# Four one-sign units become two two-sign units in a fused Fourier mixing and SoLU kernel on one core

## The chip, the cores and the metric

The kernel runs on one core of a Trainium2 chip. The metric is the time of one execution in device microseconds; shown is the median of several runs. The profile is of one execution, and its times are counted from the first instruction.

The engines are named as in the profile: PE is TensorE, DVE is VectorE, ACT is ScalarE, POOL is GpSimd, SP is SyncE, which here only issues DMAs. Each of them carries out its instructions in the order in which the program hands them over.

## The reference

```python
def _attn_ref(x):                      # x: 8 x 3136 x 256
    X = np.fft.fft(x, axis=1)
    X = np.fft.fft(X, axis=2)
    return X.real.astype(np.float32)

def _moe_ref(x, w_in, w_out, g_ln):    # x: 25088 x 256, d_ff 1024
    h = x @ w_in
    h_max = np.max(h, axis=-1, keepdims=True)
    e = np.exp(h - h_max)
    sm = e / (np.sum(e, axis=-1, keepdims=True) + 1e-09)
    solu = h * sm
    mu = np.mean(solu, axis=-1, keepdims=True)
    var = np.mean((solu - mu) ** 2, axis=-1, keepdims=True)
    ln = (solu - mu) / np.sqrt(var + 1e-06) * g_ln
    return (ln @ w_out).astype(np.float32)
```

The real part of a two-dimensional Fourier transform of each of 8 batches is taken as 25088 rows of 256, and each row goes through an up projection to 1024, a softmax times its own argument, a normalisation and a down projection to 256. All in float32.

## The kernel before

The sequence length is 3136 = 49 x 64. A frequency is k1 + 49 k2, with k1 from 0 to 48 and k2 from 0 to 63. The transform over 49 (`transform1`) and the transform over 64 with twiddle factors (`transform2`) run on PE. The batches are taken in four pairs.

**Units.** A unit is one pair of batches and one k1: 2 x 64 = 128 rows, one per partition. Since the input is real, the row of frequency -k follows from that of k: both have the same part even in the feature index and opposite odd parts. So k1 runs only from 0 to 24 (`NK` = 25), and a unit with k1 above 0 handles its rows with both signs of the odd part: 256 output rows. For k1 = 0 the mirrored rows lie in the same unit, so that unit has one sign: 128 output rows. There are 100 units, 96 with two signs and 4 with one (0, 25, 50 and 75).

**What a unit does.** PE multiplies its transform `q` by the folded input weights into two PSUM tiles `h0` and `h1` (`up`, L289). DVE adds the middle column to the first (`even`, L302, the column `r` having been spread over the partitions by a small DMA, L264) and makes the sums and differences with the second (`join`, L310, one per sign). ACT takes the exponential (`expo`, L318), DVE the product (`product`, L325), ACT the sum of squares (`square`, L332). Both signs lie in one tile `both`. DVE transposes it in blocks of 32 (`turn_both`, L396) into `v`, and sixteen DMAs per two units, issued by SP, place the blocks in `uT` (`move_blocks`, L432). POOL forms sums of quarters of `uT` (`sums`, L465), and PE multiplies by the output weights in seven products of quarters (`Down`, L472). ACT and DVE scale the results out of PSUM, and DMAs of SP (first sign, L567 and L569) and POOL (second sign, L559) store them. ACT copies one intermediate result inside PSUM as a start value ahead of the sixth of the seven products (`seed`, L498). A one-sign unit multiplies in the plain way (`down`, L542), without POOL's sums.

**Two units are a batch** (class `Batch`; not a batch of the input). A batch that is `shared` keeps the two units' blocks side by side so that the output leaves in larger DMAs. The first two batches, the last one, and every one with a one-sign unit are not shared.

**The order** is written out by hand, as one loop. In step i the engines work on the up projection of unit i, the second transform of unit i + 2 and the down projection of unit i - 5. In every even step the blocks of the two units before are moved. The first five steps (0 to 4) have an order of their own, in which PE transposes the units (`turn_whole`) instead of DVE and the DMAs; unit 0's down projection is in step 5. While one pair's units run, the first transform of the next pair runs in half pieces, at steps that the table `SUMS` names; the loads, folds and the four-part turn of its result (`turn`, POOL's DMAs into `g`) stand at steps counted from `NK`. The kernel ends with a last batch that is moved in smaller pieces.

The lines that set this rhythm:

```python
units = [Unit(p, k1) for p in range(NP) for k1 in range(NK)]
SUMS = [None] + [[f + 2 * c for c in range(NC)] for f in (3, 27, 53)]
# in step i, after the sums of POOL:
if i % 2 == 0 and whole < i - 1 < len(units) - 2:
    batches[i//2 - 1].place()
    move_blocks(batches[i//2 - 1], slice(0, 2))
```

Of the kernel before, what the change touches and what calls it, by code (L numbers as in the profile page):

```python
# [21 lines left out]
NK = N1 // 2 + 1  # L22
NH = N2 // 2
# [12 lines left out]
MIDDLE = (5,)  # L36
BY_PE = (0, 2)


def shared(b, n):  # L40

    return WHOLE // 2 <= b < n - 1 and all(u % NK for u in (2 * b, 2 * b + 1))


@with_exitstack
def kernel(
# [29 lines left out]
    out_k = out.rearrange("(p k2 k1) d -> p k1 k2 d", p=NP, k1=N1)  # L76

# [18 lines left out]
    ones = const.tile([P, P], FP32, name="ones")  # L96
    ident = const.tile([P, P], FP32, name="ident")
    neg_half = const.tile([P, 2], FP32, name="neg_half")
    idx = const.tile([P, NP * (NC + NK)], I32, name="idx")
    w_mid = const.tile([P, FF], FP32, name="w_mid")  # L100
    g_ln = const.tile([P, KF], FP32, name="g_ln")
    wbar = const.tile([P, D], FP32, name="wbar")
    top_bit = const.tile([P, 1], I32, name="top_bit")
# [139 lines left out]
    def transform2(pr, k1, bank=0):  # L243
# [3 lines left out]
        i, k = divmod(k1, KG)  # L247
        g = pr.g[i]
        table = T[0][:, :, k, :] if i == 0 else T[1][:, :, k1 - KG, :]
# [18 lines left out]
    class Unit:  # L268


        def __init__(self, p, k1):
            self.p, self.k1 = p, k1
            self.signs = (0, 1) if k1 else (0,)
            self.h, self.u, self.ot = [None] * 2, [None] * 2, [None] * 2
# [8 lines left out]
    def up(t, c):  # L283

        ps = ps_h.tile([P, FF], FP32, tag=f"h{c}", name=f"ps_h{c}")
        whole_even = c == 0 and t.p == 0 and t.k1 in MIDDLE
# [9 lines left out]
    def even(t, ps):  # L296

        t.ev = fpool.tile([P, FF], FP32, tag="ev", name="ev", bufs=1)
        if t.p == 0 and t.k1 in MIDDLE:
            nc.scalar.copy(t.ev, ps)  # L300
            return
# [19 lines left out]
    def product(t, s):  # L321

        if s == 0:
# [36 lines left out]
    class Batch:  # L360


        def __init__(self, b):
            self.first, self.shared = 2 * b, shared(b, NP * NK // 2)
# [38 lines left out]
    def turn_whole(t, late=False):  # L403
# [4 lines left out]
        for s in t.signs:  # L408
            for half in range(2):
                ps = result(2 * s + half + 1).rearrange("p (c k) -> p c k", c=n)  # L410
# [4 lines left out]
                if s or late:  # L415
# [138 lines left out]
    def store(t, s):  # L554

        dmas = []
        if s:
            i = NP * NC + t.p * NK + t.k1
# [4 lines left out]
        elif t.batch.shared:  # L563
            for j in range(4 if t.w else 0):
                a, w = divmod(j, 2)
                rows = out_k[t.p, t.k1 - 1 + w, 64 * a : 64 * a + 64].rearrange("(h n) d -> n h d", h=2)
                dmas.append(nc.sync.dma_start(out=rows, in_=t.batch.out[32 * j : 32 * j + 32]))  # L567
        else:
            dmas.append(nc.sync.dma_start(out=out_k[t.p, t.k1], in_=t.ot[s]))  # L569
# [197 lines left out]
    SUMS = [None] + [[f + 2 * c for c in range(NC)] for f in (3, 27, 53)]  # L767

    def ahead(pr, i, work, after=None):

        for c in range(NC):
            a = i - SUMS[pr.p][c]
            if work == "load" and (i == (pr.p - 1) * NK and c < 2 and (c or pr.p == 1) or a == 2 and c + 2 < NC):
                load(pr, c if a != 2 else c + 2)
# [11 lines left out]
    def ahead_pe(pr, i):  # L786

        for c in range(NC):
            half = i - SUMS[pr.p][c] - 2
            if c == 0 and pr.p == 2:  # L790
                halves = {1: (0, 1)}.get(half, ())
            else:
                halves = (half,) if half in (0, 1) else ()
# [388 lines left out]
```

## Time and profile before

| what | value |
|---|---|
| median of 3 runs | 1116.52 us (1116.32 to 1117.78) |
| profiled execution: span from first to last instruction | 1115.0 us (the profile gives no other time of it) |
| PE busy | 1098.1 us, 98% of the span |
| DVE, ACT, POOL busy | 976.0, 798.3, 808.6 us |
| first up projection starts | 48.26 us |
| step 5 starts | 78.23 us |
| up projection of the last unit starts | 1068.68 us |
| mean granted PE clock | 0.998 |

The 40 slices of the page show PE at 9 tenths or more from the third slice to the last but one. Where PE never waits, a step is as long as its instructions on PE; where it waits, the profile names what ended the wait. A table of windows gives for each stretch its length, then the busy time and number of instructions of PE, PEld, DVE, ACT and POOL, then the granted PE clock, the DMA engines' share and GB/s.

### The profile page before, as it was taken

To read this page: it belongs to the slowest core of one execution; us is meant where nothing else is said; L and a number is where in the kernel's file an instruction comes from. 1 tells how busy PE (TensorE), PEld (TensorE's weight loads), DVE (VectorE), ACT (ScalarE), POOL (GpSimd) and SP (SyncE) were. 2 spreads that over 40 slices of the span, in tenths; PEclk is the share of its full clock that TensorE was granted. 3 is DMA by queue.
4 is the path that set the end of the run, shared out by engine and by line. 5 is a ranking of instruction groups with operands and counts; after the bars stand their busy time and mean duration, and the time that the engine had idled before them with its cause. 6 is when DMAs were issued, how large, how long until landed. Compare 5 with 4: busy or idle time off the path is not lost. (4 is left out here: it accounts for less than half of the span.)

```text
span 1115.0 us, 22065 instructions
## 1 busy us (share of the span) xinstructions
PE 1098.1 (98%) x7063; PEld 877.4 (79%) x7063; DVE 976.0 (88%) x1432; ACT 798.3 (72%) x1947; POOL 808.6 (73%) x709
## 2 busy tenths in 40 slices
PE   8899999999999999999999999999999999999998
PEld 5558787888887878788788778787887788778888
DVE  7998889898888988989889989898898898998884
ACT  5598777777767777777767777777776777777772
POOL 4168888867876979766878878885775676766665
PEclk9999999999999999999999999999999999999999
DMA  9655987757968979765898888776696785865665
GB/s 338 216 175 135 185 206 176 175 135 152 193 155 180 200 181 198 177 151 130 157 176 176 194 185 197 183 174 150 139 163 141 142 169 113 163 141 114 141 132 129
DMA packets 457930, 187.76 MB, mean 168 GB/s; under 512 B 424646, under 2 KB 439254, under 8 KB 457816
## 3 DMA queue, kind: packets, MB, share of 16 engines
q1 hardware_dynamic: 443800, 146.94, 62.1%
q0 software_dynamic: 14016, 39.40, 12.9%
q8 instruction: 58, 0.95, 0.4%
q14 instruction: 56, 0.46, 0.1%
HBM read 46.75 MB, written 38.80 MB: 77 GB/s over the span
## 5 line engine op out<-in xcount | busy, mean ns | idle before, releaser
L289 PE MATMUL ps_h<-Wi,q 128*128 128x512 f32 x800 | 361.6, 593 | 0.4 <-DVE nmax L310 0.2
L465 POOL TENSOR_TENSOR S<-uT 128x512 f32<-128x512 f32 x186 | 237.3, 1276 | 110.9 <-DVE u L325 35.9
L472 PE MATMUL ps_m<-Ws,S 128*128 128x128 f32 x2304 | 296.0, 275 | 0.0
L472 PEld LDWEIGHTS ps_m<-Ws,S 128*128 128x128 f32 x2304 | 279.5, 192 | 3.2 <-issue 0.2
L332 ACT ACTIVATE h<-u,usum 128x1024 f32<-128x1024 f32 x196 | 225.0, 1148 | 73.5 <-DVE u L325 67.3
L289 PEld LDWEIGHTS ps_h<-Wi,q 128*128 128x128 f32 x800 | 144.2, 190 | 144.9 <-issue 141.9
L325 DVE SCALAR_TENSOR_TENSOR u<-h,u 128x1024 f32<-128x1024 f32 x196 | 234.9, 1234 | 10.9 <-ACT u L318 10.8
L318 ACT ACTIVATE u<-h,nmax 128x1024 f32<-128x1024 f32 x196 | 223.3, 1141 | 2.4 <-DVE nmax L310 1.1
L396 DVE STREAM_TRANSPOSE v<-u 128x2048 f32<-128x2048 f32 x88 | 203.4, 2311 | 3.1
L472 PE MATMUL ps_m<-Wo,uT 128*128 128x128 f32 x1536 | 203.7, 276 | 0.0
L472 PEld LDWEIGHTS ps_m<-Wo,uT 128*128 128x128 f32 x1536 | 187.9, 192 | 1.0 <-issue 1.0
L310 DVE CUSTOM_DVE_ANT_0 h<-ev,ps_h 128x1024 f32<-128x1024 f32 x100 | 122.1, 1221 | 17.0 <-DVE ev L302 9.1
L310 DVE CUSTOM_DVE_ANT_0 h<-h,ps_h 128x1024 f32<-128x1024 f32 x96 | 117.2, 1221 | 14.2 <-ACT ot L516 0.5
L559 POOL DMA_INDIRECT out_dram<-ot,idx x96 | 109.0, 1135 | 27.0 <-issue 11.9
L465 POOL TENSOR_TENSOR S<-uT,S 128x512 f32<-128x512 f32 x93 | 118.8, 1277 | 7.2
L465 POOL TENSOR_TENSOR S<-S,uT 128x512 f32<-128x512 f32 x93 | 118.6, 1276 | 7.3
L302 DVE SCALAR_TENSOR_TENSOR ev<-w_mid,r,ps_h 128x1024 f32<-128x1024 f32 x99 | 122.8, 1241 | 0.3
L472 PE MATMUL ps_m<-Ws,uT 128*128 128x128 f32 x768 | 101.8, 276 | 0.0
L472 PE MATMUL ps_m<-Wo,S 128*128 128x128 f32 x768 | 101.4, 275 | 0.0
L253 PEld LDWEIGHTS ps_m<-T,g 128*128 128x128 f32 x400 | 60.0, 191 | 48.1 <-issue 45.9
L507 ACT ACTIVATE ot<-ps_m,rs 128x256 f32<-128x256 f32 x96 | 45.4, 473 | 71.0 <-PE ps_m L472 50.7
L472 PEld LDWEIGHTS ps_m<-Ws,uT 128*128 128x128 f32 x768 | 93.8, 192 | 0.0
(122 smaller groups left out, 1218.1 us busy)
## 6 DMA issues: line engine op xcount, KB each, us to landing
uT<-v SPq DMA_DIRECT2D x752, 128.0 KB
g<-zd POOLq DMA_DIRECT2D x72, 160.0 KB, 4.5
out_dram<-ot SPq DMA_DIRECT2D x176, 64.0 KB
zd<-z SPq DMA_DIRECT2D x24, 400.0 KB
xa<-in_x_dram SPq DMA_DIRECT2D x24, 392.0 KB
raw_in<-in_moe_w_in_dram SPq DMA_DIRECT2D x4, 512.0 KB
xa<-in_x_dram SPq DMA_DIRECT2D x4, 512.0 KB
room<-in_x_dram SPq DMA_DIRECT2D x4, 512.0 KB
```

The lines of the kernel that those rows point to most:

```text
L253: nc.tensor.matmul(o, g[:, k, h * P : (h + 1) * P], table, start=(h == 0), stop=True, skip_group_check=True)
L289: nc.tensor.matmul(ps[:, fs], t.q[:, c * P : (c + 1) * P], Wi[:, c, fs], start=True, stop=not whole_even)
L302: nc.vector.scalar_tensor_tensor(out=t.ev, in0=w_mid, scalar=t.r, in1=ps, op0=ALU.mult, op1=ALU.add)
L310: nc.vector.tensor_tensor_reduce(out=t.h[s], in0=t.h[0] if s else t.ev, in1=t.odd, scale=1.0 if s else -0.5, scalar=3.0e38, op0=ALU.add, o ...
L318: nc.scalar.activation(out=t.u[s], in_=t.h[s], func=ACT.Exp, bias=t.nmax[:, s : s + 1], scale=-1.0, accum_out=t.esum[:, s : s + 1])
L325: t.last = nc.vector.scalar_tensor_tensor(out=t.u[s], in0=t.h[s], scalar=-1.0, in1=t.u[s], op0=ALU.mult, op1=ALU.mult, accum_out=t.usum[:, ...
L332: nc.scalar.activation(out=t.h[s], in_=t.u[s], func=ACT.Square, bias=t.usum[:, s : s + 1], scale=-float(FF), accum_out=t.ssq[:, s : s + 1])
L396: nc.vector.transpose(out=t.batch.v[:, :, t.w], in_=t.both.rearrange("p s (g n) -> p (s g) n", n=32))
L465: i = engine.tensor_tensor(out=S[j], in0=a, in1=b, op=op)
L472: nc.tensor.matmul(o, a[:, c], b[:, c], start=start and c == 0, stop=c == n - 1, skip_group_check=True)
L507: nc.scalar.mul(out=self.t.ot[1], in_=self.PP, mul=self.rs[1])
L559: dma = nc.gpsimd.indirect_dma_start(out=out, out_offset=bass.IndirectOffsetOnAxis(ap=idx[:, i : i + 1], axis=0), in_=t.ot[s], in_offset=None)
```

## The change

The four units with k1 = 0 go. Their rows are gathered into two units with two signs. In the pair tables k1 = 0 is moved to the end (index 24, `NU`); each pair has 24 ordinary units. At steps 24, 46, 70 and 86 (`SELF_STEPS`) an extra second transform yields the k1 = 0 rows of one pair; ACT copies k2 = 0 to 31 of both its batches into one half of a tile kept for them (`q_self`, in the place of `wbar` and of `ones` and `ident`, whose readers have finished), and k2 = 32, frequency 1568, which is its own mirror, into `q_half`. Two units, each with four batches by 32 frequencies, stand at places 90 and 91 (`SELF_AT`). Frequency 0 is its own mirror too; so in the second sign the rows of partitions 0, 32, 64 and 96 are free, and the eight rows of frequency 1568 go there. These eight rows run alone on 8 partitions in steps 87 to 89 (class `Half`), and DMAs of SP copy four of them into the tile `both` of each of the two units, between its product of the second sign, which now comes first, and its transpose. Their statistic is copied in the same way.

There are 98 units, all with two signs. All batches but the first two and the last are shared. Unit 0 has two signs in the steps of the start; its down projection stays plain, once for each sign.

The diff, cut to this (the tables of factors and of row numbers follow the new order and are left out):

```diff
+NU = NK - 1
+SELF_AT = 90
+SELF_STEPS = (24, 46, 70, 86)
 def shared(b, n):
-    return WHOLE // 2 <= b < n - 1 and all(u % NK for u in (2 * b, 2 * b + 1))
+    return WHOLE // 2 <= b < n - 1
+def order_of(NP):
+    units = [(p, k, None) for p in range(NP) for k in range(NU)]
+    units[SELF_AT:SELF_AT] = [(NP - 1, NU, m) for m in range(NP // 2)]
+    return units
...
-            self.signs = (0, 1) if k1 else (0,)
+            self.signs, self.usum = (0, 1), None
...
     def turn_whole(t, late=False):
-                ps = result(2 * s + half + 1).rearrange("p (c k) -> p c k", c=n)
+                bank = (1, 2, 0, 1)[2 * s + half] if late else 2 * s + half + 1
+                ps = result(bank).rearrange("p (c k) -> p c k", c=n)
...
-                if s or late:
+                if s or late and half:
                     t.wait.append((uT[:, half * n : (half + 1) * n, :, s], ps))
...
-    SUMS = [None] + [[f + 2 * c for c in range(NC)] for f in (3, 27, 53)]
+    SUMS = [None] + [[f + 2 * c for c in range(NC)] for f in (3, 26, 50)]
...
+    def gather_self(p):
+        ps = transform2(pairs[p], NU).rearrange("p (h b k) -> p h b k", h=KD, b=2)
+        of, b = q_self[p // 2].rearrange("p (h b k) -> p h b k", h=KD, b=4), p % 2 * 2
+        nc.scalar.copy(of[:, :, b : b + 2], ps[..., 0:NH])
+        nc.scalar.copy(q_half[:, :, 2 * p : 2 * p + 2], ps[..., NH])
+    class Half:
+        def spread(self):
+            nc.sync.dma_start(out=self.row[:, 0:1], in_=q_half[0:1, 1])
+        def up(self):
+            self.ps = ps_h.tile([P, FF], FP32, tag="h0", name="ps_h0")[0:B]
+            # two matmuls of q_half[:, 0] with Wi[:, 0]
+        def even(self): ...      # DVE, 8 x 1024, into a tile of xpool
+        def join(self): ...      # DVE
+        def expo(self): ...      # ACT
+        def product(self): ...   # DVE
+        def square(self): ...    # ACT
+        def stats(self): ...     # ACT, two small ones
+        def give(self, t, to, of):
+            nc.sync.dma_start(out=to, in_=of[4 * t.m : 4 * t.m + 4])
+        def give_u(self, t):
+            self.give(t, t.both[0 : P : NH, 1], self.u)
+        def give_v(self, t):
+            self.give(t, t.v[0 : P : NH, 1:2], self.row[:, 5:6])
...
         def by_seven(i):
-            return 0 <= i < len(units) and len(units[i].signs) == 2
+            return 1 <= i < len(units)
...
+            if i == NU - 3:
+                turn_parts(pairs[1], -3)
...
                 stats(prv)
+                if prv.m is not None:
+                    half.give_v(prv)
...
                 other_pairs(i, ahead_pe)
+                if i in SELF_STEPS:
+                    gather_self(SELF_STEPS.index(i))
+                if i == SELF_STEPS[-1]:
+                    half = Half()
+                    half.spread()
+                if i == SELF_STEPS[-1] + 1:
+                    half.up()
...
+            if i == SELF_STEPS[-1] + 1:
+                half.even()
+                half.join()
...
-                for s in cur.signs:
+                if i == SELF_STEPS[-1] + 2:
+                    half.expo()
+                for s in cur.signs if cur.m is None else (1, 0):
                     product(cur, s)
+                    if cur.m is not None and s:
+                        half.give_u(cur)
+                if i == SELF_STEPS[-1] + 2:
+                    half.product()
+                if i == SELF_STEPS[-1] + 3:
+                    half.square()
+                    half.stats()
```

Lines of the kernel after are 14 or more higher: L302 is L316, L310 is L324, L325 is L339, L332 is L346, L396 is L410, L432 is L447, L472 is L487.

Where the change puts its instructions is seen in the order of the built programs. First DVE at the start. Before, from unit 0's even part to unit 1's products (`ISA` is the join and the reading of its minimum):

```order
L302 SCALAR_TENSOR_TENSOR ev<-w_mid,r,ps_h_432 128x1024
L310 ISA h,nmax<-ev,ps_h_437 128x1024
L310 ISA nmax 128x1
L644 SCALAR_TENSOR_TENSOR Wo<-raw_out,g_ln,S_105 128x256 x2
L302 SCALAR_TENSOR_TENSOR ev<-w_mid,r,ps_h_453 128x1024
L325 SCALAR_TENSOR_TENSOR u,usum<-h,u 128x1024
L310 ISA h,nmax<-ev,ps_h_458 128x1024
```

And the same place now:

```order
L316 SCALAR_TENSOR_TENSOR ev<-w_mid,r,ps_h_432 128x1024
L324 ISA h,nmax<-ev,ps_h_437 128x1024
L324 ISA nmax 128x1
L324 ISA h,nmax<-h,ps_h_437 128x1024
L324 ISA nmax 128x1
L662 SCALAR_TENSOR_TENSOR Wo<-raw_out,g_ln,S_105 128x256 x2
L316 SCALAR_TENSOR_TENSOR ev<-w_mid,r,ps_h_456 128x1024
L339 SCALAR_TENSOR_TENSOR u,usum<-h,u 128x1024 x2
L324 ISA h,nmax<-ev,ps_h_461 128x1024
```

One more join stands ahead of unit 1's even part, and one more product ahead of its joins.

Second, DVE in step 87, from the even part of unit 87 to its transpose. Before:

```order
L302 SCALAR_TENSOR_TENSOR ev<-w_mid,r,ps_h_8484 128x1024
L310 ISA h,nmax<-ev,ps_h_8489 128x1024
L310 ISA nmax 128x1
L310 ISA h,nmax<-h,ps_h_8489 128x1024
L310 ISA nmax 128x1
L530 SCALAR_TENSOR_TENSOR ot_8421<-ps_m_102,rs_8209,ot_8421 128x128
L533 SCALAR_TENSOR_TENSOR ot_8498<-ps_m_104,rs_8209,ot_8498 128x256
L325 SCALAR_TENSOR_TENSOR u,usum<-h,u 128x1024 x2
L396 STREAM_TRANSPOSE v_8483<-u 128x64x32
```

Now (8x1024 are the eight rows; `ps_h_8795` lies in the same PSUM tile `h0` as the unit's own):

```order
L316 SCALAR_TENSOR_TENSOR ev<-w_mid,r,ps_h_8760 128x1024
L324 ISA h,nmax<-ev,ps_h_8765 128x1024
L324 ISA nmax 128x1
L324 ISA h,nmax<-h,ps_h_8765 128x1024
L324 ISA nmax 128x1
L545 SCALAR_TENSOR_TENSOR ot_8774<-ps_m_102,rs_8556,ot_8774 128x128
L548 SCALAR_TENSOR_TENSOR ot_8775<-ps_m_104,rs_8556,ot_8775 128x256
L844 SCALAR_TENSOR_TENSOR half<-w_mid,half,ps_h_8795 8x1024
L849 ISA half<-half 8x1024
L849 ISA half 8x1
L339 SCALAR_TENSOR_TENSOR u,usum<-h,u 128x1024 x2
L410 STREAM_TRANSPOSE v_8650<-u 128x64x32
```

The even part and the join of the eight rows stand behind the two rows that take the last products of the step out of PSUM, and ahead of the unit's own products.

Third, SP from step 88 to step 92. `uT<-v` x16 are the block moves of an even step, `out_dram<-ot` the stores of a batch, `r<-` the spread of a middle column. Before:

```order
L432 DMA uT<-v_8483 32x16x64 x16
L567 DMA out_dram<-ot_8606 32x2x256 x4
L264 DMA r<-q 128x1x1 x2
L432 DMA uT<-v_8668 32x16x64 x16
L567 DMA out_dram<-ot_8786 32x2x256 x4
L264 DMA r<-q 128x1x1 x2
L432 DMA uT<-v_8848 32x16x64 x16
```

Now (the moves of step 90 are those of `v_8843`):

```order
L585 DMA out_dram<-ot_8774 32x2x256 x4
L278 DMA r<-ones_ident 128x1x1
L278 DMA r<-q 128x1x1
L447 DMA uT<-v_8843 32x16x64 x16
L872 DMA u<-half 4x1024
L585 DMA out_dram<-ot_8956 32x2x256 x4
L278 DMA r<-q 128x1x1
L872 DMA own<-half 4x1
L872 DMA u<-half 4x1024
L278 DMA r<-q 128x1x1
L872 DMA own<-half 4x1
L447 DMA uT<-v_9021 32x16x64 x16
```

The copy of four rows into unit 90 stands behind the sixteen moves of step 90; the copy into unit 91 stands behind the stores of step 91 and ahead of the moves of step 92.

More of the change, by code (lines that the diff above doesn't have):

```diff
@@ L772, in ahead @@
             a = i - SUMS[pr.p][c]
-            if work == "load" and (i == (pr.p - 1) * NK and c < 2 and (c or pr.p == 1) or a == 2 and c + 2 < NC):
+            if work == "load" and (i == (pr.p - 1) * NU and c < 2 and (c or pr.p == 1) or a == 2 and c + 2 < NC):
                 load(pr, c if a != 2 else c + 2)
@@ L881 @@
         weights.keep_in(KD, middle)
-        units = [Unit(p, k1) for p in range(NP) for k1 in range(NK)]
+        units = [Unit(i, *u) for i, u in enumerate(order_units)]
         for i in (1, 2):
@@ L886 @@
         weights.mean_out(0)
-        pairs_q = [(t, transform2(pairs[0], t.k1, t.k1)) for t in units[:2]]
+        pairs_q = [(t, transform2(pairs[0], t.k, t.k)) for t in units[:2]]
         confine(weights.units[0], parts=(0, 1))
```

110 lines of the change are left out of this document (78 added, 32 removed).

## The prediction, made before the changed kernel ran

> **What bounds the kernel now.** I read the head of the page first, then the TensorE timeline around a one-sign unit, then a table of windows cut at the starts of the steps, and last the queues of VectorE, ScalarE and SyncE inside one step. The page has TensorE busy for 98% of the span.
>
> ```profile
> span 1115.0 us, 22065 instructions
> PE 1098.1 (98%) x7063; PEld 877.4 (79%) x7063; DVE 976.0 (88%) x1432; ACT 798.3 (72%) x1947; POOL 808.6 (73%) x709
> ```
>
> The timeline shows what a step is on TensorE: it starts with the eight up-projection rows (L289) of one unit and ends with the seven products (L472) of the unit five steps older.
>
> ```profile
> 868.42 3.60 PE L289 MATMUL ps_h<-Wi,q 128*128 128x512 f32 x8
> ...
> 874.18 1.95 PE L472 MATMUL ps_m<-Ws,S 128*128 128x128 f32 x16
> ...
> 878.70 3.60 PE L289 MATMUL ps_h<-Wi,q 128*128 128x512 f32 x8
> 882.13 0.61 PE L253 MATMUL ps_m<-T,g 128*128 128x128 f32 x4
> 882.58 3.62 PE L542 MATMUL ps_m<-Wo,uT 128*128 128x256 f32 x16
> ```
>
> From start to start this gives 3.44 us for the eight up rows (878.70 to 882.13), 0.44 for the second transform (L253), and 3.46 for the plain product of a one-sign unit (L542, up to the next step at 886.04). The row of sixteen holds the fifth and the sixth of the seven products, 0.89 each; the sixth is due about 6.6 into a step.
>
> The windows are the steps (length first, then each engine's busy time). The first two are steps 5 and 6, the others a step with half a first transform (368.53), a bare step (896.86), and those around the three one-sign units.
>
> ```profile
> 78.23:89.17 10.94, 10.66 (x37) 6.37 (x38) 10.49 (x17) 9.69 (x23) 8.64 (x9) 1.00 0.01 1
> ...
> 346.60:356.59 9.99, 9.31 (x38) 6.35 (x37) 9.44 (x15) 5.04 (x12) 7.75 (x6) 1.00 1.15 229
> 356.59:368.53 11.94, 11.24 (x73) 8.95 (x72) 9.06 (x13) 10.62 (x28) 8.22 (x8) 1.00 0.67 153
> 368.53:379.53 11.00, 11.00 (x74) 8.91 (x73) 10.14 (x18) 7.76 (x23) 10.51 (x11) 1.00 1.05 209
> ...
> 621.50:632.93 11.43, 11.38 (x73) 8.96 (x72) 10.93 (x18) 9.62 (x27) 10.44 (x9) 1.00 0.82 201
> 868.42:878.70 10.28, 10.28 (x71) 8.37 (x69) 9.14 (x12) 8.10 (x19) 6.36 (x7) 1.00 0.94 192
> 878.70:886.04 7.34, 7.34 (x30) 5.11 (x29) 6.93 (x8) 4.36 (x10) 2.51 (x2) 1.00 0.99 177
> 886.04:896.86 10.82, 10.61 (x70) 8.21 (x68) 9.30 (x13) 8.85 (x23) 10.06 (x10) 1.00 0.66 143
> 896.86:906.99 10.13, 10.13 (x70) 8.22 (x69) 9.78 (x15) 7.79 (x22) 7.45 (x9) 1.00 0.92 164
> ```
>
> A bare step is 10.13 us of pure TensorE work, half a first transform adds 0.87, a one-sign unit's step is 7.34. But VectorE is busy 9 to 10 of these 10.13 us: whatever is put on it, or holds it up, has little room.
>
> **The main loop, on TensorE.** Two whole steps go: -20.27. Three one-sign products in the loop become seven products: 3 x (10.13 - 7.34) = +8.38. The waits around them go: 0.91 (9.99 against 7.34 + 2 x 0.87) + 0.94 + 0.43 + 0.15 + 0.69 = 3.12, as -3.12. Second transforms stay at 100 (two went with the steps, four gathers come, two units need none): +0.88. Step 5 gets a second plain product for unit 0, 3.46. Its work before was 7.34 + 0.87 + 1.7 (unit 5's middle column, four more rows of the up kind) = 9.9, and it took 10.94; with 13.4 TensorE alone sets its end: +2.4. Sum: **-11.7**. The gathers' eight small copies on ScalarE, the transforms and loads moved with the 24-step rhythm (SyncE's rows, POOL's folds) and the turn of pair 1 that now stands ahead of POOL's sums are taken at nothing: ScalarE idles 0.47 ahead of the seed copy alone (row below), and each of the others has a step or so of lead. If the turn came late, step 22 would wait for it.
>
> **The start.** Unit 0 gets a second sign.
>
> ```profile
> 54.16 1.28 DVE L302 SCALAR_TENSOR_TENSOR ev<-w_mid,r,ps_h 128x1024 f32<-128x1024 f32 x1
> 55.36 1.22 DVE L325 SCALAR_TENSOR_TENSOR u<-h,u 128x1024 f32<-128x1024 f32 x1
> ...
> 57.90 1.22 DVE L310 CUSTOM_DVE_ANT_0 h<-h,ps_h 128x1024 f32<-128x1024 f32 x1 [0.17 <-ACT h L332]
> ```
>
> ```profile
> 57.90 1.15 ACT L318 ACTIVATE u<-h,nmax 128x1024 f32<-128x1024 f32 x1
> ...
> 60.57 1.13 ACT L958 COPY uT<-ps_m 128x512 f32<-128x512 f32 x2
> 61.58 1.16 ACT L332 ACTIVATE h<-u,usum 128x1024 f32<-128x1024 f32 x1
> ```
>
> VectorE has no gap here, so one more join (1.37 to the next row) and one more product (1.14) cost 2.5 at least. ScalarE is packed as well (60.57 ends where 61.58 begins): to it come an exponential, which fits in a gap, a square (1.25), two more copies of transposed halves (0.5 each) and 0.2 of statistics. Followed through: unit 0's square now starts at 57.95 instead of 56.62 behind two products; the second sign's square ends at 60.5, its first copy at 61; the last four transposes wait for that copy's bank, and unit 1's exponential, which overwrites what they read, for them: 61.75 instead of 57.90. Unit 1's chain is then 3.9 late (61.75 against 57.90), and the same three terms, a square, a copy and a bank, push unit 2's to between 5 and 6; from there on both engines keep the rhythm they had. I take **+5.7**, with 2.5 as the lower end and 7 as the upper.
>
> **The eight rows (steps 87 to 89).** In an ordinary step VectorE and ScalarE run like this:
>
> ```profile
> 936.88 0.35 DVE L530 SCALAR_TENSOR_TENSOR ot<-ps_m,rs,ot 128x128 f32<-128x128 f32 x1
> 937.59 0.48 DVE L533 SCALAR_TENSOR_TENSOR ot<-ps_m,rs,ot 128x256 f32<-128x256 f32 x1 [0.37 <-PE ps_m L472]
> 938.00 1.22 DVE L325 SCALAR_TENSOR_TENSOR u<-h,u 128x1024 f32<-128x1024 f32 x1
> ...
> 940.40 2.31 DVE L396 STREAM_TRANSPOSE v<-u 128x2048 f32<-128x2048 f32 x1
> 942.64 1.24 DVE L302 SCALAR_TENSOR_TENSOR ev<-w_mid,r,ps_h 128x1024 f32<-128x1024 f32 x1
> ```
>
> ```profile
> 940.40 1.15 ACT L332 ACTIVATE h<-u,usum 128x1024 f32<-128x1024 f32 x1
> ...
> 941.55 0.35 ACT L259 COPY q<-ps_m 128x256 f32<-128x256 f32 x1
> 942.36 0.25 ACT L498 COPY ps_m<-ps_m 128x128 f32<-128x128 f32 x1 [0.47 <-PE ps_m L472]
> ```
>
> No row shows eight partitions by 1024; I price them as 128 by 1024, since the same count passes along each partition. The up rows cost half of 3.44, 1.7, and wait some 0.5 for the bank that the unit's own even part frees. Their even part stands on VectorE behind the L533 row, which ends 0.6 after the step's last product; 1.24 later the bank is free, and the next unit's up rows need that same bank: TensorE idles 1.9. Together 4.1. The join and product (1.2 each) are then absorbed by VectorE's 0.5 to 1 us of room per step, and the 1.9 of ScalarE rows in step 89 may push the seed copy (L498) 0.5 late: **+4.6**. The lower end is the bare 1.7.
>
> **The copies (steps 90 and 91).** The row of SyncE is the point of this forecast. Step 90 starts at 977.92.
>
> ```profile
> 977.92 3.60 PE L289 MATMUL ps_h<-Wi,q 128*128 128x512 f32 x8
> ```
>
> ```profile
> 966.24 13.87 SPq L432 DMA_DIRECT2D uT<-v  x16
> ...
> 986.51 13.59 SPq L432 DMA_DIRECT2D uT<-v  x16
> 1000.21 2.91 SPq L567 DMA_DIRECT2D out_dram<-ot  x4
> ```
>
> Every second step SyncE issues sixteen block moves for 13.6 us, from 8.6 into the even step (they wait for a buffer that the fourth product frees) to 22.2, which is 12 us into the next one. Unit 90's copy of four rows is issued behind all sixteen, at 22.2; its data are ready at about 12, the product rows following the L533 row above, which follows the step's last product at 10.1. Landing: a row DMA issued at 48.23 releases VectorE at 50.32.
>
> ```profile
> 48.23 0.55 SPq L264 DMA_DIRECT2D r<-q  x1
> ```
>
> ```profile
> 50.32 1.28 DVE L302 SCALAR_TENSOR_TENSOR ev<-w_mid,r,ps_h 128x1024 f32<-128x1024 f32 x1
> ```
>
> ```profile
> DMA to landing us min/median/max: 4.2/4.5/5.7
> ```
>
> The last row is POOL's loads of g, 160 KB, the upper end; four 4 KB rows are nearest to the first, 2.0 to 2.2, so 24.4. Until then VectorE's transpose (due at 13.1, 940.40 being 2.8 behind 937.59) and ScalarE's second square stand still, and all that is queued behind them. ScalarE's chain after it is square 1.15, copy of q 0.37, seed 0.25: the seed for step 91 is written at 26.2. TensorE needs it for the sixth product, due at 10.13 + 6.6 = 16.7: a wait of 9.5. VectorE's chain ends beside it: transpose 2.31, even 1.4, two joins 2.75 = 30.9, when TensorE is at 31.6 with the second half of step 92's up rows. For unit 91 SyncE is free, but the delayed products end at 33.4, the copy lands at 35.4, square and seed follow at 37.8, and step 92's sixth product was due at 36.5: 1.2 more. **+10.7**; with the upper landing time 13.5. The two little DMAs of the last statistic hold ScalarE's mix copies for about a microsecond in step 92, which delays an exponential and no product.
>
> A wait this long touches the clock.
>
> ```profile
> 10.62 5.37 PE L698 MATMUL wps<-w_in,Q 128*128 128x512 f32 x8 [3.56 <-DMA Q<-in_q_tab_dram]
> 10.62:11.63 1.01, 1.01 (x3) 0.48 (x4) 0.98 (x3) 0.94 (x3) 0.70 (x2) 1.00 1.06 327
> 11.63:15.05 3.42, 3.42 (x6) 1.36 (x5) 3.32 (x7) 2.74 (x5) 2.78 (x3) 0.50 1.01 351
> ```
>
> After 3.56 idle the granted clock (third from the end) was 0.50 for 3.42 us. One such window costs 1.7, of which the 1.2 above is then no longer waited: **+0.5**. The Trainium skill, "TensorE: Matmul & The Clock Gate", in its part on the clock gate, says that the array falls to half clock after an idle window of about 3.4 us and comes back after a busy one. By that rule the slow stretch after a wait of this length can reach two windows, and the sum would be 1.7 higher than mine; this trace shows one window.
>
> **The sum.** -11.7 + 5.7 + 4.6 + 10.7 + 0.5 = +9.8 against the profiled span of 1115.0. The runs' median, 1116.52, lies 1.5 above that span, so I forecast **1126.3**.
>
> **Rivals.** First, the copies are cheap. If the sixteen moves were issued 10 us earlier in their step, or the copy stood ahead of them, it would land before 15 and only 1 to 2 us would be left: -11.7 + 5.7 + 4.6 + 1.5, about 1116.6; with the lower ends of start and eight rows, -11.7 + 2.5 + 1.7 + 1.5, 1110.5. What decides is whether the moves start before 0 of the even step; the rows at 966.24 and 986.51, 8.6 in, speak against it. Second, the start and the eight rows at their low ends, the copies as forecast: -11.7 + 2.5 + 1.7 + 10.7 + 0.5 = +3.7, 1120.2; the packed ScalarE speaks against. Third, more stalls: copies landing at 4.5 us, two slow windows, a start of 7, or the turn of pair 1 late: 1131 to 1134. That the change doesn't do what it says I exclude: 98 units stand in the order.
>
> **How the numbers follow.** Forecast, 1121 to 1130: 0.6. Copies cheap, 1109 to 1118: 0.18. Low ends, 1118 to 1121: 0.1. More stalls: 0.12. The range that leaves out about 2 in 10 is 1116 to 1131. One measurement tells 0.2%, 2.2 us, from no change. Below 1114.3 lies half of the cheap case and a little more, 0.12; within, to 1118.8, 0.1; slower 0.78.
>
> **What would show it.** Step 5 starting near 84 instead of 78.23; step 87 lasting 14; the row of four rows on SyncE issued after sixteen moves; ScalarE's square and VectorE's transpose both waiting some 10 us for that copy, and a TensorE gap of that size in the step after. If the gap is under 3, the forecast is wrong.

## The result, and the profile after

| | before | changed |
|---|---|---|
| median of the runs, us | 1116.84 (1116.32 to 1117.78) | 1143.22 (1141.19 to 1148.1) |
| ratio, 95% interval | | 1.0244, 1.022 to 1.0269 |
| span of the profiled execution, us | 1115.0 | 1139.4 |

The change makes the kernel 2.4% slower; 1126.3 was forecast. The profiled execution is the fastest of the four. The head of the changed kernel's page shows the same work on PE, spread over 24 us more:

```profile
PE 1097.0 (96%) x7083; PEld 877.5 (77%) x7083; DVE 999.3 (88%) x1432; ACT 802.5 (70%) x1969; POOL 818.7 (72%) x711
```

In the changed kernel the lines have moved: `up` is L303, the seven products L487, the first transform L239, the copies of `q` and of the seed L273 and L513, product and square L339 and L346, the transpose L410, the loads of x L142 (SP) and L144 (POOL), the mirror add L160, the folds L167, L168 and L192, POOL's sums L480, the block moves L447, the copies of the eight rows L872. Rows of the table of windows, for steps 5, 30 to 33, 87, 91 and 92 (columns as before):

```profile
82.70:96.57 13.87, 13.87 (x53) 9.59 (x54) 11.69 (x19) 9.69 (x23) 11.57 (x13) 1.00 0.08 20
356.03:367.02 10.99, 10.99 (x74) 8.90 (x73) 9.79 (x15) 7.56 (x22) 4.78 (x5) 1.00 0.86 174
367.02:378.63 11.61, 11.24 (x74) 8.96 (x73) 11.05 (x13) 8.56 (x20) 10.95 (x12) 1.00 1.00 175
378.63:391.17 12.54, 11.24 (x74) 8.96 (x73) 12.19 (x16) 7.58 (x23) 8.17 (x6) 1.00 0.96 196
391.17:403.97 12.80, 11.24 (x75) 8.96 (x73) 12.45 (x16) 8.53 (x20) 12.04 (x10) 1.00 0.96 174
976.43:990.91 14.48, 12.38 (x74) 8.57 (x73) 10.97 (x15) 9.14 (x20) 7.90 (x7) 1.00 0.96 173
1020.73:1042.43 21.70, 11.84 (x71) 9.77 (x69) 9.30 (x13) 8.01 (x19) 7.84 (x7) 0.76 0.67 120
1042.43:1052.56 10.13, 10.13 (x70) 8.22 (x69) 8.15 (x10) 6.76 (x20) 5.31 (x5) 1.00 0.03 5
```

In step 5 PE never waits, step 87 waits for the eight rows, step 91 for their copy. But steps 31 to 33 were to last 11.00 like step 30, and do not. They lie in the window of pair 2's first transform, where VectorE is now busy for up to 12.45 us instead of 9.79. Thirteen steps in the windows of pairs 2 and 3 are longer in this way: 7.6 us in pair 2's, 7.0 in pair 3's. Pair 1's window has none of it.

Of the 24.4 us between the spans, 14.6 lie there; the copies take 11.8 (21.70 - 10.13, and 0.24 in step 90), the start 5.2, the eight rows 4.4, the tail 0.5; up to the first up projection 0.75 is gained. The rest, the main loop, is -11.4.

**The waits nobody forecast.** Rows of the table of waits over the whole execution (us in total, times, longest), before:

```profile
ACT h L332 <- DVE u L325: 67.3, 82, 2.2
POOL xa L146 <- DMA out_dram<-ot: 4.5, 4, 3.4
```

And in the changed kernel:

```profile
ACT h L346 <- DVE u L339: 103.3, 92, 3.9
POOL xa L160 <- DMA out_dram<-ot: 30.5, 8, 6.1
POOL xa L160 <- DMA xa<-in_x_dram: 21.0, 6, 6.6
PE ps_m L239 <- ACT q L273: 11.5, 13, 1.6
```

POOL's mirror add waits 51 us for loads of x. (The releaser in the first of these rows is another DMA on SyncE's queue, but the load of `xa` stands there as well, and in pairs 2 and 3 all twelve adds that waited in this way start 4.4 to 6.9 us after their load was issued.) PE's 13 waits in the first transforms are for ScalarE's copy of `q` out of the bank they share. That copy stands behind ScalarE's square, and the square waits for VectorE's product: 30.3 and 30.5 us in the windows of pairs 2 and 3, where it was 14.8 and 13.8 before. What makes the product late is in VectorE's groups. These are the folds of pair 2 (minimum, median, maximum in ns):

```profile
L167 DVE TENSOR_TENSOR y<-xa x16: 411/417/1110, 334.6 to 507.2; 98x254 f32<-98x254 f32 x16
L168 DVE TENSOR_TENSOR y<-xa x16: 409/419/1499, 335.0 to 507.5; 98x254 f32<-98x254 f32 x16
L192 DVE TENSOR_TENSOR y<-xa,xb x16: 150/155/1223, 335.3 to 507.9; 98x2 f32<-98x2 f32 x15, 98x1 f32<-98x1 f32 x1
```

The same row of L168 takes 0.41 or 1.5 us. The timelines of VectorE and POOL in step 32 show when:

```profile
379.38 0.85 DVE L167 TENSOR_TENSOR y<-xa 98x254 f32<-98x254 f32 x1
380.16 1.48 DVE L168 TENSOR_TENSOR y<-xa 98x254 f32<-98x254 f32 x1
381.56 1.22 DVE L192 TENSOR_TENSOR y<-xa,xb 98x2 f32<-98x2 f32 x1
```

```profile
378.68 1.27 POOL L480 TENSOR_TENSOR S<-S,uT 128x512 f32<-128x512 f32 x1
380.03 1.33 POOL L480 TENSOR_TENSOR S<-uT,S 128x512 f32<-128x512 f32 x1
381.32 1.44 POOL L480 TENSOR_TENSOR S<-uT 128x512 f32<-128x512 f32 x1
...
388.90 1.26 POOL L160 TENSOR_TENSOR xa<-xa,xb 98x510 f32<-98x510 f32 x1 [4.07 <-DMA out_dram<-ot]
```

The fold rows end with a POOL row or 0.3 us after it (382.78 and 382.76; 381.64 and 381.36). POOL's sums belong before this point; they are late because the mirror add ahead of them was. The kernel means to keep them apart: `behind` ties the mirror add and the first of POOL's sums to the last product of the unit before ("two operands at a time from SBUF"), and before the change the adds waited 38.6 us for that product, now 18.3. And SyncE shows why the load was late:

```profile
365.48 18.63 SPq L447 DMA_DIRECT2D uT<-v  x16
384.54 0.34 SPq L142 DMA_DIRECT2D xa<-in_x_dram  x1
```

The table `SUMS` names the step of a chunk's first mirror add. Its folds begin one step later, its first transform two steps later, and in that step stands the load of the chunk after next. (The account of the order above counts all loads and folds from `NK`; that holds for the first two loads of a pair alone.) With starts at 3, 27 and 53 these loads stand in odd steps, which issue no block moves; with 26 and 50 those of pairs 2 and 3 stand in even steps, behind all sixteen moves. In time: before the change a load left SyncE 4.3 to 6.9 us into the step ahead of the one whose add reads it; now it leaves between 0.6 us before and 5.9 us after the start of the very step that reads it (384.54 is 5.9 into step 32). That is theory A: parity of the starts, through SyncE's queue.

**The copies.** SyncE around step 90, and the waits for it:

```profile
1019.18 13.83 SPq L447 DMA_DIRECT2D uT<-v  x16
1033.11 0.59 SPq L872 DMA_DIRECT2D u<-half  x1
```

```profile
DVE v L410 <- DMA uT<-v: 10.4, 1, 10.4
PE ps_m L487 <- issue: 9.9, 1, 9.9
ACT h L346 <- DMA u<-half: 9.0, 1, 9.0
```

### The profile page after: what moved, and what is told of

The parts are those of the page before. It is cut to its first block, busy times and chain, and to the rows that moved or that the text cites. A ratio compares the mean times of both kernels' runs of the same rounds, so it can differ in the third digit from the quotient of the medians.

```text
span 1139.4 us, 22100 instructions
## 1 busy us (share of the span) xinstructions
PE 1097.0 (96%) x7083; PEld 877.5 (77%) x7083; DVE 999.3 (88%) x1432; ACT 802.5 (70%) x1969; POOL 818.7 (72%) x711
## 5 line engine op out<-in xcount | busy, mean ns | idle before, releaser
L303 PE MATMUL ps_h<-Wi,q 128*128 128x512 f32 x768 | 347.0, 593 | 2.5 <-DVE half L844 1.8
L480 POOL TENSOR_TENSOR S<-uT 128x512 f32<-128x512 f32 x188 | 243.3, 1294 | 113.5 <-DVE u L339 38.2
L487 PE MATMUL ps_m<-Ws,S 128*128 128x128 f32 x2328 | 301.6, 276 | 9.9 <-issue 9.9
L346 ACT ACTIVATE h<-u,usum 128x1024 f32<-128x1024 f32 x196 | 224.9, 1148 | 112.3 <-DVE u L339 103.3
L487 PEld LDWEIGHTS ps_m<-Ws,S 128*128 128x128 f32 x2328 | 284.1, 192 | 14.2 <-issue 10.2
L303 PEld LDWEIGHTS ps_h<-Wi,q 128*128 128x128 f32 x768 | 138.3, 190 | 140.9 <-issue 138.9
L339 DVE SCALAR_TENSOR_TENSOR u<-h,u 128x1024 f32<-128x1024 f32 x196 | 233.1, 1225 | 14.1 <-ACT u L332 14.1
L332 ACT ACTIVATE u<-h,nmax 128x1024 f32<-128x1024 f32 x196 | 223.5, 1142 | 4.7 <-DVE nmax L324 2.5
L410 DVE STREAM_TRANSPOSE v<-u 128x2048 f32<-128x2048 f32 x92 | 212.6, 2311 | 14.6 <-DMA uT<-v 10.4
L487 PE MATMUL ps_m<-Wo,uT 128*128 128x128 f32 x1552 | 206.1, 276 | 0.0
L487 PEld LDWEIGHTS ps_m<-Wo,uT 128*128 128x128 f32 x1552 | 190.4, 193 | 1.9 <-issue 1.9
L324 DVE CUSTOM_DVE_ANT_0 h<-ev,ps_h 128x1024 f32<-128x1024 f32 x98 | 119.7, 1221 | 17.7 <-DVE ev L316 9.2
L324 DVE CUSTOM_DVE_ANT_0 h<-h,ps_h 128x1024 f32<-128x1024 f32 x98 | 119.7, 1221 | 15.6 <-DVE nmax L324 1.5
L574 POOL DMA_INDIRECT out_dram<-ot,idx x98 | 113.4, 1157 | 26.9 <-issue 12.1
L480 POOL TENSOR_TENSOR S<-uT,S 128x512 f32<-128x512 f32 x94 | 120.6, 1283 | 7.3
L480 POOL TENSOR_TENSOR S<-S,uT 128x512 f32<-128x512 f32 x94 | 120.0, 1277 | 7.4
L316 DVE SCALAR_TENSOR_TENSOR ev<-w_mid,r,ps_h 128x1024 f32<-128x1024 f32 x97 | 120.3, 1241 | 0.4 <-PE ps_h L303 0.3
L160 POOL TENSOR_TENSOR xa<-xa,xb 98x510 f32<-98x510 f32 (+1 forms) x48 | 59.4, 1238 | 70.3 <-DMA out_dram<-ot 30.5
L487 PE MATMUL ps_m<-Ws,uT 128*128 128x128 f32 x776 | 102.7, 275 | 0.0
L487 PE MATMUL ps_m<-Wo,S 128*128 128x128 f32 x776 | 102.5, 275 | 0.0
L487 PEld LDWEIGHTS ps_m<-Ws,uT 128*128 128x128 f32 x776 | 94.7, 192 | 0.0
```

Source lines behind the costliest of these rows:

```text
L160: i = engine.tensor_tensor(out=a[:, :, 1:D], in0=a[:, :, 1:D], in1=rb[:, :, D - 1 : 0 : -1], op=ALU.add)
L303: nc.tensor.matmul(ps[:, fs], t.q[:, c * P : (c + 1) * P], Wi[:, c, fs], start=True, stop=not whole_even)
L316: nc.vector.scalar_tensor_tensor(out=t.ev, in0=w_mid, scalar=t.r, in1=ps, op0=ALU.mult, op1=ALU.add)
L324: nc.vector.tensor_tensor_reduce(out=t.h[s], in0=t.h[0] if s else t.ev, in1=t.odd, scale=1.0 if s else -0.5, scalar=3.0e38, op0=ALU.add, o ...
L332: nc.scalar.activation(out=t.u[s], in_=t.h[s], func=ACT.Exp, bias=t.nmax[:, s : s + 1], scale=-1.0, accum_out=t.esum[:, s : s + 1])
L339: t.last = nc.vector.scalar_tensor_tensor(out=t.u[s], in0=t.h[s], scalar=-1.0, in1=t.u[s], op0=ALU.mult, op1=ALU.mult, accum_out=t.usum[:, ...
```

## The experiments

**Starts back to odd steps.**

```diff
-    SUMS = ... for f in (3, 26, 50)]
+    SUMS = ... for f in (3, 25, 49)]
```

> The changed kernel with pairs 2 and 3 starting their sums at steps 25 and 49 (odd) instead of 26 and 50 (even); all else as changed. Theory A (queue): with even starts the loads of x are issued on SyncE behind the sixteen block moves of the same even step, POOL's mirror adds wait for them, and POOL's sums run over VectorE's folds in the next step. With odd starts the loads stand in a step without moves: TensorE's waits in the first-transform windows of pairs 2 and 3 (about 14.6 us) go, 1143.2 - 14.6 = about 1128.5. Theory B (the moved gathers and the turn of pair 1 cause the waits, not the starts): no change, 1141 to 1145.

Measured: 1127.54 us (ratio to before 1.0096, 1.0079 to 1.0112), 15.7 below the changed kernel. Every step of the two windows lasts 11.00, apart from the last of each at 11.45; the folds of pair 2:

```profile
L167 DVE TENSOR_TENSOR y<-xa x16: 411/414/802, 326.5 to 491.1; 98x254 f32<-98x254 f32 x16
L168 DVE TENSOR_TENSOR y<-xa x16: 410/416/418, 327.2 to 491.4; 98x254 f32<-98x254 f32 x16
```

From 150 us on none of the 45 L168 rows takes over 0.42 us, as in the kernel before (44 rows of L154). Theory B falls: gathers and the turn of pair 1 are as they were. Of theory A this run shows the parity; SyncE's rows fit the queue, for a load now leaves 4.4 us into step 30 (358.53) and is read in step 31:

```profile
345.99 13.36 SPq L447 DMA_DIRECT2D uT<-v  x16
...
362.95 0.51 SPq L142 DMA_DIRECT2D xa<-in_x_dram  x1
```

The run also puts the rest of the kernel where the prediction had it: 1127.5 against 1126.3.

**The kernel before with even starts.**

```diff
-    SUMS = ... for f in (3, 27, 53)]
+    SUMS = ... for f in (3, 26, 52)]
```

> The kernel before with pairs 2 and 3 starting at steps 26 and 52 instead of 27 and 53, nothing else changed. Theory A (queue): the same waits appear without the rest of the change, 7.0 to 7.6 us for each pair, 1116.8 + 14.6 = about 1131. Theory B: 1116 to 1118, no new waits; at most 1 us, since the starts alone matter to nothing.

Measured: 1135.70 us (1.0174, 1.0157 to 1.0191). The starts alone cost 19 us, 4 more than A expected. The two runs together also rule out that an earlier start is what counts: one step earlier gained there and costs here. In the windows table step 31 stands out, right behind the plain product of unit 25 in step 30:

```profile
357.90:375.97 18.07, 14.41 (x74) 11.48 (x72) 15.18 (x18) 11.15 (x29) 16.87 (x13) 0.81 0.83 174
```

It is 6.1 us longer than the same step of the kernel before (11.94). POOL had stood still for 11.7 us waiting for a load, and behind PE's wait the granted clock was 0.81 in this step: PE is busy 14.41 us with what takes 11.24 at full clock. These 3.2 us are most of the 4 that A did not expect.

**The loads on another queue, and in the middle of the moves.** Two ways to bring the load forward with even starts. First:

```diff
-        nc.sync.dma_start(out=xa[0:rows], ...)
+        (nc.gpsimd if pr.p > 1 else nc.sync).dma_start(out=xa[0:rows], ...)
```

> The changed kernel, starts at 26 and 50 as they are, but the plain loads of x of pairs 2 and 3 are issued by POOL instead of SyncE, at the same places of the program. Theory A (the load stands behind the moves in SyncE's queue): the mirror adds run at about 4 to 5 us into their step again, and most of the 14.6 us go; POOL issues one more DMA every second step, about 1 us of its time, so 1129 to 1132. Theory C (an even start is bad by itself, because the folds and the first transforms then share a step with other work, and the late load is only a companion): waits stay, 1141 to 1146.

Second, in even steps after the fold:

```diff
-                move_blocks(batches[i // 2 - 1], slice(0, 2))
+                move_blocks(batches[i // 2 - 1], slice(0, 2), groups=(0, 1))
...
+                other_pairs(i, ahead, "load")
+                move_blocks(batches[i // 2 - 1], slice(0, 2), groups=(2, 3))
...
```

> The changed kernel with its even starts, all loads of x still on SyncE, but in the even steps the load is issued after eight of the sixteen block moves instead of after all of them (so some 7 us earlier, about 5 us into the next step). POOL issues nothing more than in the changed kernel. Theory A (the load's place behind the moves is the cause): the mirror adds come back to about 4 us into the step, VectorE's fold rows to 0.41 us, and nearly all of the 14.6 us of waits go: 1128 to 1131. Theory C (an even start is bad in itself, and moving the load to POOL helped by half for some other reason): 1138 to 1146.

Measured: 1134.98 us (1.0162, 1.0141 to 1.0183) and 1135.12 (1.018, 1.0159 to 1.0201): 8 us gained in each, about half, between A and C in both. SyncE with the load on POOL, and then with the load between the moves:

```profile
369.50 19.86 SPq L447 DMA_DIRECT2D uT<-v  x16
```

```profile
364.84 7.37 SPq L447 DMA_DIRECT2D uT<-v  x8
372.32 1.12 SPq L142 DMA_DIRECT2D xa<-in_x_dram  x1
373.48 10.42 SPq L447 DMA_DIRECT2D uT<-v  x8
```

In the windows of pairs 2 and 3 sixteen moves take 13.2 to 16.3 us with odd starts. Here they take 16.3 to 20.2 with the load on POOL and 15.0 to 18.4 with the load between them (its own issue not counted), and the load now runs beside them. The moves fall behind their step, and with the load on POOL its sums wait for `uT` five times, 8.9 us in pair 2. So POOL's sums still slide over the folds: 12 and 8 of the 45 L168 rows take 1.48 to 1.50 us. One wait has become another: behind the moves the load is late, beside them the moves are. This is theory F, and the next run tests it by itself.

**A load beside the moves, for nobody.** On the kernel with odd starts, in even steps of pairs 2 and 3:

```diff
+            if i == 2 and extra is not None:    # after eight block moves
+                for k in range(2):
+                    nc.sync.dma_start(out=spare[k], in_=x_pn[0:PR, 1 : CH + 1, :])
```

> The changed kernel with odd starts (25 and 49), whose sixteen block moves take 13 to 14.5 us in most steps, with two more transfers of the size of a load of x (400 KB each, to a place in DRAM that nobody reads) issued on SyncE after the eighth block move of every even step of pairs 2 and 3. Nothing waits for their data. Theory F: a load that runs beside the block moves stretches them, and that is why issuing the load earlier (from POOL, or between the moves) brought only half: the moves last 16 to 20 us, POOL's sums wait for uT, and 3 to 9 us of TensorE waits appear in the windows of pairs 2 and 3: 1131 to 1137. If transfers beside the moves cost them nothing but the two issues (about 1 us each on SyncE), the moves take about 15 to 16 us with the issues and the time stays at 1127.5.

Measured: 1147.01 us (1.0285, 1.0257 to 1.0314), 19.5 us above the kernel without them, more than F expected. SyncE, and step 38, one of those that pay (1.6 us of it to the clock):

```profile
415.60 7.42 SPq L451 DMA_DIRECT2D uT<-v  x8
423.07 1.72 SPq L448 DMA_DIRECT2D spare<-in_x_dram  x2
424.83 9.72 SPq L451 DMA_DIRECT2D uT<-v  x8
```

```profile
446.67:462.91 16.24, 12.86 (x74) 10.55 (x73) 14.80 (x18) 8.09 (x24) 12.08 (x9) 0.89 0.99 197
```

Transfers beside the moves stretch them, with odd starts too: in the fourteen steps with spare transfers sixteen moves take 15.8 us in the median without the two issues, against 13.9 in the same steps of the kernel without, and POOL's sums wait 25.3 us for `uT` in the two windows. Since these are two transfers where a load is one, and also write to DRAM, which a load of x does not, the size does not carry over to it.

**The copies on POOL.**

```diff
-            nc.sync.dma_start(out=to, in_=of[4 * t.m : 4 * t.m + 4])
+            nc.gpsimd.dma_start(out=to, in_=of[4 * t.m : 4 * t.m + 4])
```

> The changed kernel, but the copies of the eight rows into units 90 and 91 (rows and statistic) are issued by POOL instead of SyncE. If the 11.6 us by which step 91 is longer come from the row copy standing behind sixteen block moves, step 91 goes to 10.1 to 12 us, the wait of 9.9 us on TensorE and the half clock behind it go, and the time falls by 10 to 12 us to about 1132. If the wait is the landing time of the copy itself or the reordered products, step 91 stays above 18 us.

Measured: 1137.80 us (1.0187, 1.017 to 1.0204), 5.4 below the changed kernel, half of what was expected. Step 91 falls to 11.85, so the wait was for the queue; but step 92 rises from 10.13 to 14.39 (and the late loads cost 17.4 us in this profile, not 14.6). POOL's timeline shows the new wait, the statistic's copy, with the sums behind it:

```profile
1028.30 0.66 POOL L872 DMA_DIRECT2D u<-half  x1 [1.61 <-DVE u L339]
1033.76 0.57 POOL L872 DMA_DIRECT2D own<-half  x1 [4.80 <-ACT own L361]
1034.36 1.29 POOL L480 TENSOR_TENSOR S<-uT 128x512 f32<-128x512 f32 x1
```

These sums run until 1039.58. VectorE's product of unit 91 beside them takes 2.03 us instead of 1.22, unit 91's row copy leaves behind them at 1041.61, and PE waits 2.40. Another 1.6 of the step are clock: PE is busy 11.99, at a granted clock of 0.88, where the same products take 10.37 at full clock.

**Odd starts, only the row copies on POOL.**

```diff
+    SUMS = ... for f in (3, 25, 49)]
-            self.give(t, t.both[0 : P : NH, 1], self.u)
+            nc.gpsimd.dma_start(out=t.both[0 : P : NH, 1], in_=self.u[4 * t.m : 4 * t.m + 4])
```

> The changed kernel with starts 25 and 49, and the row copies of units 90 and 91 issued by POOL while their statistics stay on SyncE. With the copies on POOL and the statistics too, steps 91 and 92 were 1.7 and 4.3 us longer than a bare step; in step 92 POOL's sums stood 4.8 us behind the copy of a statistic. If that is the reason for the 4.3, with the statistics on SyncE some 2 us per step are left, the landing time of the copy: 1127.5 - 12.2 + 4 = about 1119. If the wait in step 92 is from the copies themselves, 6 us stay: about 1121.5.

Measured: 1118.29 us (1.0017, 1.0008 to 1.0027). Steps 91 and 92 last 14.10 and 10.13, so the statistic's copy was what held step 92. The sum, 4 us above bare, came out as expected by luck: not 2 us of landing in each step, but a wait of 2.10 in step 91 and, behind it, half clock (PE busy 12.00, granted clock 0.88).

**The eight rows through a bank of their own.** To the kernel just shown:

```diff
-            self.ps = ps_h.tile([P, FF], FP32, tag="h0", name="ps_h0")[0:B]
+            self.ps = result(0)[0:B]    # 512 columns in step 87, 512 in step 88
...     # join in step 88, exponential and product in 89, square and statistics behind unit 90's squares
```

> As the kernel with odd starts and row copies on POOL, but the eight rows go through a bank of their own in two halves of 512 (steps 87 and 88, join in 88, exponential in 89, square in 90) instead of through the bank of the units' even part. If the 2.5 us that step 87 waits are for that bank, they go: step 87 from 14.48 to about 11.0, step 88 from 9.76 to 10.6, 2.6 us in all, about 1116.5. If VectorE's time is what the eight rows cost, step 88 or 89 becomes longer instead and the time stays.

Measured: 1118.76 us (1.0016, 1.0007 to 1.0026): no gain. Steps 87 to 90 gain 2.0 us (87 goes from 14.49 to 11.28), so the bank was a wait of that size; step 91 goes from 14.10 to 16.21 and takes it back. ScalarE's timeline in step 91:

```profile
1012.10 1.15 ACT L346 ACTIVATE h<-u,usum 128x1024 f32<-128x1024 f32 x1 [1.30 <-DMA u<-half]
...
1013.25 1.13 ACT L863 ACTIVATE half<-half 8x1024 f32<-8x1024 f32 x1
...
1014.89 0.34 ACT L273 COPY q<-ps_m 128x256 f32<-128x256 f32 x1
1015.14 0.25 ACT L513 COPY ps_m<-ps_m 128x128 f32<-128x128 f32 x1
```

The eight rows' square, moved one step on by the edit, stands between the square that waits for the copy and the seed. (The profile names POOL's sums as what ended PE's wait of 4.21 here. But the sums of a step are for the products of the next, and PE starts at 1015.49, 0.1 after the seed's row ends.)

**The transpose behind the even part.** To that:

```diff
+                    even(cur, up(cur, 0))
+                    if units[i - 1].m is not None:
+                        turn_both(units[i - 1])
...
```

> As the kernel with the bank of its own, and for units 90 and 91 alone VectorE's transpose stands behind the next unit's even part, so that the even part (1.24 us) runs while the row copy lands. If VectorE standing still for the copy's landing (about 2 us in each of two steps) is what is left of the copies' cost, 1 to 2.5 us go: about 1114.5, a little below the kernel before. If ScalarE's square, which waits for the same copy, is what counts, no change.

Measured: 1118.95 us (1.0021, 1.0012 to 1.003), step 91 at 16.04: no change, as expected if ScalarE is what counts.

**The eight rows' square ahead.** To the kernel with the bank, `half.square()` and `half.stats()` of step 90 ahead of the products:

```diff
+                if i == SELF_STEPS[-1] + 4:
+                    half.square()
+                    half.stats()
                 for s in cur.signs if cur.m is None else (1, 0):
                     product(cur, s)
...
```

> As the kernel with the bank of its own, but in step 90 the eight rows' square and statistics (1.7 us on ScalarE) stand ahead of unit 90's products and squares, where ScalarE stood idle for 2.5 us, instead of behind them. In that kernel the bank gained 2.0 us in steps 87 to 90 and step 91 lost 2.1. Theory D: it was lost because these 1.7 us stand between the square that waits for the row copy and the copies that TensorE needs next; then step 91 goes from 16.2 to 14.1 us or less and the time from 1118.8 to about 1116.5. Theory E: step 91 waits for POOL's sums, which stand behind the row copy in POOL's queue; then no change.

Measured: 1116.33 us (1.0, 0.999 to 1.0009). Theory D holds: steps 91 and 92 are 12.18 and 11.42, together 2.7 less. Of these, 1.6 are the clock, which stays at 1.00 (PE busy 10.37 in step 91 instead of 12.00).

**The square first, then the copy.** To that, for units 90 and 91:

```diff
+                        square(cur, s)      # s == 1, right behind its product
                         half.give_u(cur)
...
                     join(cur, s)
+                    if s == 0 and units[i - 1].m is not None:
+                        turn_both(units[i - 1])
...
```

> As the kernel with the square ahead, and for units 90 and 91: the square of the second sign comes right behind its product and the row copy is issued after it (so ScalarE waits for no copy), and VectorE's transpose stands between the next unit's two joins instead of ahead of its even part. If the wait left in step 91 is ScalarE and VectorE standing still while the copy lands, it goes: step 91 from 14 to 10.1 to 11 us, about 1113 in all, below the kernel before (1116.6). If it is POOL's sums behind the copy (theory E), step 91 stays at 14 us or more.

Measured: 1112.85 us (0.9971, 0.996 to 0.9981), 0.3% below the kernel before, with the interval below 1. The windows of steps 91 and 92:

```profile
1004.01:1014.55 10.54, 10.37 (x70) 8.29 (x69) 8.60 (x12) 8.44 (x20) 6.95 (x8) 1.00 0.91 155
1014.55:1025.19 10.64, 10.37 (x70) 8.21 (x69) 9.78 (x14) 8.11 (x22) 6.79 (x7) 1.00 0.50 95
```

The copies cost 0.9 us where they cost 11.8. Theory E falls a second time: POOL's sums still stand behind the copy, and PE's waits in these two steps are 0.17 and 0.27.

## Why the prediction was wrong, and where it was right

**The step that failed** is the sentence that takes "the transforms and loads moved with the 24-step rhythm (SyncE's rows, POOL's folds)" at nothing because "each of the others has a step or so of lead". The loads have two steps between their place in the program and their reader, but SyncE's queue takes them: the new starts moved the loads from odd to even steps, behind the block moves whose 13.6 us the prediction itself had put in front of the row copies, and a load now leaves about when the step that reads it starts. The prediction followed one DMA through SyncE's queue and let the loads pass at nothing: they cost 14.6 us, in no rival and outside the range.

The lateness had to cross three engines to reach PE: POOL's add waits for the load, its sums slide over VectorE's folds, those take 1.48 instead of 0.41 us, and ScalarE's square and copy of `q` come late behind VectorE's product. The Trainium skill, "SBUF — State Buffer", in its part on who interferes with whom, says that a VectorE instruction with two SBUF inputs contends with a GpSimd one that reads SBUF. These rows agree: counted over the changed kernel's trace from 150 us on, all 14 L168 rows that overlap a POOL sum or mirror add take 1.48 to 1.50 us, all 31 others 0.28 to 0.42.

**The rest** of the sum came within 0.1 of its 9.8, and in part by luck: the terms below are off by up to 0.6 both ways, the tail adds 0.5, and 0.75 is gained ahead of the first up projection, which starts anywhere from 46.90 to 49.16 in the profiles of these runs.

**The main loop**, forecast at -11.7, came to -11.4 as what is left of the span.

**The start**, 5.7, took 5.2: from unit 0's up projection to step 5 it is 35.2 us (47.51 to 82.70) against 30.0 before (48.26 to 78.23). The chain is the one described: the last four transposes of unit 0 wait 1.05 for ScalarE's copy, and unit 1's exponential starts 3.8 later than before, counted from the first up projection (60.99 - 47.51 against 57.90 - 48.26; forecast 3.9). In step 5, 13.87, PE never waits, as forecast (13.4). No experiment touched the start.

**The eight rows**, 4.6, took 4.4, nearly all in step 87. PE waited 0.26 and 1.85 for the bank (forecast 0.5 and 1.9), and the own bank took 2.0 out of these steps.

**The copies**, 10.7 and 0.5 for the clock, took 11.8. The place in the queue was right (issued at 1033.11, 12.4 into step 91, forecast 12), and both engines and PE waited as described. PE's wait was 9.9 where 9.5 was forecast. The prediction priced one slow window at 1.7 and let it swallow the second wait, of 1.2; so it came, for step 92 lasts 10.13, and the slow clock cost 1.5 (half of 3.08) to 1.7 (PE busy 11.84 in step 91 against 10.13). The windows from the fall of the clock on show it (granted clock third from the end):

```profile
1030.16:1037.32 7.16, 0.00 (x1) 0.04 (x1) 1.67 (x1) 1.77 (x5) 1.37 (x2) 0.50 0.80 150
1037.32:1040.40 3.08, 3.08 (x14) 3.08 (x15) 2.91 (x3) 1.33 (x5) 0.00 (x0) 0.50 0.02 0
1040.40:1042.43 2.03, 2.03 (x21) 2.03 (x19) 1.70 (x5) 1.59 (x4) 0.00 (x0) 1.00 0.00 0
```

Of 10.24 slow microseconds PE worked in 3.08. Two slow windows after the wait, which the prediction reckoned possible by the rule of the Trainium skill, "TensorE: Matmul & The Clock Gate", in its part on the clock gate, would have doubled the price; less than one came.

What stays open: how much of a load's harm beside the moves is the DMA engines' time and how much SyncE's queue; whether an even start costs something by itself as well (theory C), since no run with even starts got more than about half of the time back; and why the waits differ between executions of the same steps (17.4 us of them stand in the profile with the copies on POOL, 14.6 in the changed kernel's).

## What to carry to other kernels

When a rhythm of n steps is laid over another with period two, write down which residue each DMA falls on before and after: a shift by one step put a 392 KB load behind sixteen block moves and cost more than anything the change was about. A load had two bad places here, behind a burst on its queue and beside it; moving it from one to the other gave back half. A copy that stalls in-order engines is paid by whatever stands behind it there, so put the reader that does not need the copied rows ahead of it.

## What the runs showed of the hardware

A VectorE row of 2 elements per partition, 0.15 us alone, took 1.22 us beside a POOL row of 1.44 and ended with it (382.78 and 382.76); all eight such rows that overlap one took 1.22. So the cost here went by the other row, not by its own size. The eight rows' square took 1.13 us on 8 partitions by 1024, where the square of 128 by 1024 took 1.15, and VectorE's join of them 1.21 against 1.22, so these few rows by themselves were as dear as a full tile. Sixteen block moves of the same size took between 13 and 20 us to issue, the longest with a load beside them. And a short wait was enough for half clock: with the row copies on POOL alone PE waited 2.10 us until 1014.78, and from 1015.43 on the granted clock was 0.50 for 3.41 us, all of which fell on work.
